# A 96-byte tile at the right edge of the on-chip memory, ahead of all pools on that side

## The chip, the cores and the metric

The kernel runs on one core of a Trainium2 chip. The metric is the device time of one execution in microseconds, lower is better. A core has a matrix engine (PE, with the loading of its stationary operand shown apart as PEld), a vector engine (DVE), a scalar engine (ACT), GpSimd (POOL) and SyncE (SP), whose queue issues nearly all DMAs here. The on-chip memory has 128 partitions; a tile takes the same byte range in each of them. The program's allocator gives out this range from both ends: pools opened on the left grow upwards, pools opened with `side="right"` are stacked downwards from the right edge.

## What is computed

Three layers in a row, in float32 (the weights of the second layer arrive as float64):

```python
attn_out = _attn_ref(q, k, v, centroids)        # 2 batches, 8 heads, 768 tokens, head size 64;
                                                # a query sees only keys of the same nearest centroid
x = attn_out.transpose(0, 2, 1, 3).reshape(1536, 512)
x = (sigmoid(x @ w_gate) * (x @ w_val)) @ w_out # 512 -> 1536 -> 512
p = domain_probs / (domain_probs.sum(-1, keepdims=True) + 1e-09)
out = sum(p[:, e:e+1] * (relu(x @ w1[e]) @ w2[e]) for e in range(4))   # 512 -> 1024 -> 512
```

## The kernel before

**Attention** (to about 290 us) runs over 96 items: 8 pairs of heads, each with 2 heads of 6 tiles of 128 queries. The order of all work is written out by hand (`SLOT`, `START`, `FIRST`, `TAIL`). For each item PE forms the scores `S` (L420), DVE their negated maximum (L423), ACT the exponentials `P` (L431), PE transposes `P` (`T`, L440), ACT and DVE split it in a high and a low part `ph` and `pl` (L443, L444), and PE multiplies these with `vv` (`PV`, L453 and L454). Between the items the next pair is prepared: `nq`, `nk`, `nv` are loaded, q and k are transposed (L243) and split in `hiq`, `loq`, `hik`, `lok`, which DMAs on the SP queue copy to the tiles `L` and `R` of the scores (L378 to L383).

**Gated MLP** (to about 574 us). Every float32 product is made of three passes by `mm3` (L620 to L622): high weights with high x, high weights with low x, low weights with high x. The weights are the stationary operand, 128 columns of 4 bytes, and x is the moving one. `gate` makes `pg` and `pv` from the weights `wgh`, `wgl`, `wvh`, `wvl` and the moving `X0`, `X1`: for the first two f-tiles in four pieces of 384 tokens, for the ten others in three pieces of 512 tokens. `outp` makes `po` from the stationary `woh`, `wol` and the moving `hh`, `hl`, 512 columns wide.

**Mixture** (to the end). For each of 32 f-tiles `hidden` makes three blocks `ph` of 512 tokens, 12 products each, from the stationary `w1h`, `w1l` and the moving `X0`, `X1` (which now hold the MLP's result). After each four f-tiles `outp` makes 12 blocks `po` of 12 products each, from the stationary `h2h`, `h2l` and the moving `woh`, `wol` (L802 to L804). PE takes the products in the order of the program; the weights of the coming f-tiles are loaded and split by ACT and POOL two f-tiles ahead (L762 to L765, L613, L614).

**Where the tiles lie.** On the left side: `X0`, `X1`, the constants, `L`, `R`, `P`, `ph`, `pl`, `vv`, `U`, and later `acc`, `sg`, `woh`, `wol`, `hh`, `hl`, `h2h`, `h2l`. On the right side, all through `self.right`: the pools `nat` (`nq`, `nk`, `nv`), `hl` (`hiq` and its like) and `pm` in attention; `raw` (float64 weights), `cv` and `whl` (`wgh`, `wgl`, `wvh`, `wvl`) in the MLP; `raw2` and `w1p` (`w1h`, `w1l`) in the mixture. The right edge is at byte 229,344 of a partition, which is 1,791 x 128 + 96. The matrix operands have these start addresses in the program before (the slices that one product takes start a multiple of 512 bytes further on):

| operand | role | starts at byte | left over by 128 | left over by 512 |
|---|---|---|---|---|
| `X0`, `X1` | moving | 16,768 and 41,344 | 0 | 384 |
| `woh`, `wol` | stationary in the MLP, moving in the mixture | 94,592 to 113,024 | 0 | 384 |
| `hh`, `hl`, `h2h`, `h2l` | moving in the MLP, stationary in the mixture | 115,072 to 170,368 | 0 | 384 |
| `wgh`, `wgl`, `wvh`, `wvl` | stationary | 184,288 to 198,624 | 96 | 480 |
| `w1h`, `w1l` | stationary | 208,864 to 219,104 | 96 | 480 |
| `P` (transposes) | stationary | 121,728 to 127,872 | 0 | 384 |
| `nq`, `nk` (transposes) | stationary | 220,128 and 223,200 | 96 | 480 |

In attention the left pools end at byte 183,168 and the lowest right pool begins at 183,264, so that 96 bytes are free between them.

Of the kernel before, what the change touches and what calls it, by code (L numbers as in the profile page):

```python
# [5 lines left out]
F32 = mybir.dt.float32  # L6
# [17 lines left out]
BIG = float(2.0 ** 100)  # L24
CLOW, CHIGH = 2.0, float(15 * 2 ** 29)  # bits 0x40000000 and 0x4FF00000: exponents 0 and 255 after the shift

# [4 lines left out]

# The item of a pair of heads (12 to a pair) at which a piece of its work is issued, and where within the item:
# 0 after the scores, 1 after the products with v, 2 at the end.
SLOT = {
# [7 lines left out]
AHEAD, PVLAG = 2, 2  # L42
# The engines that split parts of q, k and v.
ON = {"q0": "pool", "q1": "dve", "k0": "mix", "k1": "dve", "vhi": "act"}
# What comes before the first item: steps of the first two pairs (as pair and step), and the first items' scores.
START = [
# [5 lines left out]
]  # L52
# Items of the other steps of these two pairs that don't keep to the table.
FIRST = {
# [3 lines left out]
}  # L58
# The same, counted from the end of attention, for the first weights of the gated MLP: room, loads, steps of conversion.
TAIL = {  # L60
# [8 lines left out]
class Net:  # L69
# [37 lines left out]
    def warm(self, n):  # L107
        """Products that nobody reads: the array's clock falls to half while it waits."""
        ps = self.ps.tile([128, 384], F32, name="PV", tag="PV", bufs=1)
        for _ in range(n):  # L110
            self.nc.tensor.matmul(ps[:, 0:128], self.identb, self.identb, start=True, stop=True)

    def centroids(self, p):
        """Normalised centroids, transposed, split and laid out as the weights of the similarities."""
        nc = self.nc
        x = p.tile([128, D], F32, name="cx")
        nc.scalar.dma_start(out=x, in_=self.cent.rearrange("h c d -> (h c) d"))
        xx = p.tile([128, 2 * D], F32, name="cxx")

        def scale():  # L120
            sx = p.tile([128, D], F32, name="csx")
            nc.vector.tensor_tensor(sx, x, x, op=ALU.mult)
            sq = p.tile([128, 1], F32, name="csq")
            nc.vector.tensor_reduce(sq, sx, axis=AX.X, op=ALU.add)
            r = p.tile([128, 1], F32, name="cr")
            nc.gpsimd.tensor_tensor(r, sq, self.half[:, 0:1], op=ALU.pow)
            nc.vector.tensor_scalar(r, r, 1e-6, None, op0=ALU.add)
            nc.vector.reciprocal(r, r)
            nc.vector.tensor_scalar(xx[:, 0:D], x, r, None, op0=ALU.mult)
            nc.vector.tensor_scalar(xx[:, D:2 * D], x, r, None, op0=ALU.mult)  # L130

        def place():
            ps = self.ps.tile([128, 128], F32, name="cT", tag="T", bufs=3)
            nc.tensor.transpose(ps, xx, self.ident)
            ch = p.tile([128, 128], F32R, name="ch")
            cl = p.tile([128, 128], F32R, name="cl")
            nc.scalar.activation(ch, ps, AF.Copy)
            nc.vector.tensor_tensor(cl, ps, ch.bitcast(F32), op=ALU.subtract)
            for hh in range(2):
                rows = slice(hh * 64, hh * 64 + 64)  # L140
                for part, src in ((0, ch), (1, cl)):
                    sv = src[rows].bitcast(F32).rearrange("p (a h c) -> p a h c", a=4, h=2)[:, :, hh, :]
                    for s in range(2):
                        o = part * 64 + s * 32 + hh * 16
                        (nc.vector if part else nc.gpsimd).tensor_copy(self.cb[rows, :, s, o:o + 16], sv)

        return scale, place
# [12 lines left out]

# [1 line left out]
    def load_nat(self, src, b, pr, tag):  # L162
# [6 lines left out]
    def prep(self, n):  # L169
        """What pair n needs before its scores, as (item at which it is issued, work) in order."""  # L170
        nc = self.nc
        b, pr = self.plist[n]
        P = self.pairs[n] = {}
        first = n == 0
        x, hl = {}, {}
# [5 lines left out]

        # 1 / (norm + 1e-6) of the rows of q and k
        def square(s, m):
# [37 lines left out]
        def vsplit(hh):  # L221
            def go():
                # v as [Vh0 | Vl0 | Vl1 | Vh1]
                if hh == 0:
                    P["vv"] = self.vvp.tile([128, NT, 4, 64], F32R, name="vv", tag="vv")
                hi, lo = P["vv"][:, :, 3 * hh, :], P["vv"][:, :, 1 + hh, :]
                xv = x["v"][:, :, hh * 64:hh * 64 + 64]
                if ON["vhi"] == "act":
                    nc.scalar.activation(hi, xv, AF.Copy)
                else:  # L230
                    nc.vector.tensor_copy(hi, xv)
                nc.gpsimd.tensor_tensor(lo, xv, hi.bitcast(F32), op=ALU.subtract)
            return go
# [88 lines left out]
        def arg_first(hh):  # L322
            """The same for one head of the first pair, which nothing hides: in small pieces."""
            G = NT * 2
# [121 lines left out]
    def pv(self, n, hh, th, ph, pl):  # L446
        """One half of a head's tokens, in three pieces."""
        nc = self.nc
# [12 lines left out]
        if th == 1:  # L461
            # the two products with the halves of v meet on the head's rows
            if hh == 0:
                P["A"] = self.xsp.tile([128, S], F32, name="A", tag="A")
                P["W"] = self.xsp.tile([128, S], F32, name="W", tag="W")
            r, o = slice(hh * 64, hh * 64 + 64), slice(64 - hh * 64, 128 - hh * 64)
            nc.sync.dma_start(out=P["A"][r], in_=U[r])
            nc.sync.dma_start(out=P["W"][r], in_=U[o])

    def finish(self, n):  # L470
# [22 lines left out]

        # the vector engine has less to do once the last scores are through
        eng = nc.vector if n == len(self.plist) - 1 else nc.gpsimd
# [73 lines left out]

# [1 line left out]
    def conv64(self, raw, tag, hl_pool, put):  # L571
        """float64 bits in raw (int64) -> float32 rounded to nearest even, split in two; as steps to issue in turn."""
        nc = self.nc
        shape = list(raw.shape)
        n = shape[1] * shape[2]
# [4 lines left out]
        def magnitude():  # L580
            # a factor of 2^16 on the high word's bits as a float32 moves the exponent's bias to that of float32
            t["c"] = self.cv.tile([128, n], I32, name="cvc", tag="cvc")
            t["s"] = self.cv.tile([128, n], I32, name="cvs", tag="cvs")
            nc.scalar.activation(t["c"].bitcast(F32), hi_w.bitcast(F32), AF.Abs, scale=float(2.0 ** 16))
            nc.scalar.activation(t["s"], lo_w.bitcast(U32), AF.Copy, scale=float(2.0 ** -29))
# [31 lines left out]
    def mm3(self, ps, wh, wl, xh, xl, first, last):  # L617
        """ps += w.T @ x, float32 products from three float32r passes."""
        nc = self.nc
        nc.tensor.matmul(ps, wh, xh, start=first, stop=False)  # L620
        nc.tensor.matmul(ps, wh, xl, start=False, stop=False)  # L621
        nc.tensor.matmul(ps, wl, xh, start=False, stop=last)  # L622

# [1 line left out]
    def open_weights(self):  # L625
# [21 lines left out]
    def moe1(self):  # L647
# [61 lines left out]

        # the tokens of the first batch go first: the last pair of heads is still under way  # L710
        half = [slice(i * 384, i * 384 + 384) for i in range(4)]
# [37 lines left out]

# [1 line left out]
    def open_mixture(self):  # L751
# [6 lines left out]
    def prepare(self, i):  # L758
        """Weights of the i-th f-tile of the mixture."""
        e, f = self.tiles[i]  # L760
# [6 lines left out]
    def moe2(self):  # L767
# [20 lines left out]
        def outp(ch):  # L788
            first, last = ch == 0, ch == len(tiles) // CH - 1
            e = tiles[ch * CH][0]  # L790
            for t in range(B * NT):
                # the very last product is halved, to end sooner
                parts = (slice(0, 256), slice(256, 512)) if last and t == B * NT - 1 else (slice(0, 512),)
# [28 lines left out]
    def run(self):  # L822
# [4 lines left out]
        self.X = [self.xp.tile([128, 4, N], F32R, name=n, tag=n) for n in ("X0", "X1")]  # L827
        self.dr = es.enter_context(self.tc.tile_pool(name="dr", bufs=2, space=DRAM))
        self.right = es.enter_context(ExitStack())
        with ExitStack() as a:  # L830
            self.psS = self.pool(a, "psS", 2, PSUM)
            self.ps = self.pool(a, "ps", 1, PSUM)
            # what only the preparation of a pair uses gives way to the first weights before the last pair ends
            self.nat = self.pool(self.right, "nat", 1, side="right")
# [62 lines left out]
```

## Time and profile before

| | |
|---|---|
| time, median of 3 runs | 1111.92 us (1109.7 to 1115.82) |
| span of the profiled execution | 1109.4 us |
| time of the profiled execution beside its span | not recorded for this kernel; the fastest run lies 0.3 us above the span, the median 2.5 us |
| PE busy | 1083.7 us, 98% of the span |
| PE's weight loads busy | 920.5 us, 83% |
| DVE, ACT, POOL busy | 551.5, 425.7 and 313.9 us |
| granted PE clock, mean | 0.995 of full speed |

Products on PE overlap: a row says how long one took from its start to its modelled end, while the next one starts well before. What the stream costs is the distance from start to start, which a timeline gives: the difference of two starts divided by the number of products between them.

### The profile page before, as it was taken

To read this page: it belongs to the slowest core of one execution; us is meant where nothing else is said; L and a number is where in the kernel's file an instruction comes from. 1 tells how busy PE (TensorE), PEld (TensorE's weight loads), DVE (VectorE), ACT (ScalarE), POOL (GpSimd) and SP (SyncE) were. 2 spreads that over 40 slices of the span, in tenths; PEclk is the share of its full clock that TensorE was granted. 3 is DMA by queue.
4 is the path that set the end of the run, shared out by engine and by line. 5 is a ranking of instruction groups with operands and counts; after the bars stand their busy time and mean duration, and the time that the engine had idled before them with its cause. 6 is when DMAs were issued, how large, how long until landed. Compare 5 with 4: busy or idle time off the path is not lost.

```text
span 1109.4 us, 14146 instructions
## 1 busy us (share of the span) xinstructions
PE 1083.7 (98%) x5387; PEld 920.5 (83%) x5387; DVE 551.5 (50%) x887; ACT 425.7 (38%) x866; POOL 313.9 (28%) x267
## 2 busy tenths in 40 slices
PE   6999999998999999999999999999999999999998
PEld 5998999998988888888888888888888888888887
DVE  7999999999776355534342222222222222222222
ACT  4887888888565035404232022120211202021110
POOL 7577778834232012102021021110202102021100
PEclk8999999999999999999999999999999999999999
DMA  7677766655342112102011010010101101010002
GB/s 172 143 160 160 175 149 154 149 131 147 115 133 97 37 43 94 36 1 86 10 36 31 19 48 29 19 48 10 58 19 39 38 1 58 19 48 10 10 19 95
DMA packets 88515, 78.94 MB, mean 71 GB/s; under 512 B 42720, under 2 KB 71744, under 8 KB 88448
## 3 DMA queue, kind: packets, MB, share of 16 engines
q1 hardware_dynamic: 88016, 77.99, 27.2%
q8 instruction: 42, 0.69, 0.3%
q14 instruction: 25, 0.20, 0.1%
q10 hardware_dynamic: 432, 0.06, 0.0%
HBM read 48.29 MB, written 3.19 MB: 46 GB/s over the span
## 4 chain that ended last, share of the span: by engine, by line
PE 89%; DVE 4%; DMA 4%; SPq 1%; issue 1%; ACT 1%; POOL 0%; ACTq 0%; POOLq 0%; DVEq 0%
PE ph L620 8%; PE ph L621 8%; PE ph L622 8%; PE po L804 8%; PE po L803 8%; PE po L802 8%; PE T L440 4%; PE S L420 4%; PE po L622 3%; PE po L620 3%; PE po L621 3%; PE pg L620 3%; PE pv L622 3%; PE pg L621 3%; PE pv L621 3%; PE pv L620 3%
## 5 line engine op out<-in xcount | busy, mean ns | idle before, releaser
L785 DVE SCALAR_TENSOR_TENSOR h2l<-ph,h2h 128x512 fp32r<-128x512 f32 x96 | 66.4, 691 | 208.9 <-ACT h2h L784 208.9
L620 PE MATMUL ph<-X,w1h 128*128 128x512 f32 x384 | 152.3, 396 | 0.0
L621 PE MATMUL ph<-X,w1h 128*128 128x512 f32 x384 | 152.2, 396 | 0.0
L622 PE MATMUL ph<-X,w1l 128*128 128x512 f32 x384 | 152.2, 396 | 0.0
L802 PE MATMUL po<-woh,h2h 128*128 128x512 f32 (+1 forms) x388 | 150.1, 387 | 0.0
L803 PE MATMUL po<-wol,h2h 128*128 128x512 f32 (+1 forms) x388 | 150.1, 387 | 0.0
L804 PE MATMUL po<-woh,h2l 128*128 128x512 f32 (+1 forms) x388 | 150.1, 387 | 0.0
L809 DVE SCALAR_TENSOR_TENSOR acc<-po,pn,acc 128x512 f32<-128x512 f32 (+1 forms) x85 | 63.3, 744 | 159.1 <-PE po L804 159.1
L614 POOL TENSOR_TENSOR wol<-r,woh 128x512 fp32r<-128x512 f32 x32 | 41.5, 1306 | 271.1 <-ACT woh L613 224.8
L613 ACT ACTIVATE woh<-r 128x512 fp32r<-128x512 f32 x32 | 20.2, 631 | 240.7 <-PE po L804 207.7
L595 POOL TENSOR_TENSOR cvc<-cvc,cvs 128x512 int32<-128x512 int32 x36 | 50.3, 1401 | 202.4 <-DVE cvc L592 196.4
L444 DVE TENSOR_TENSOR pl<-T,ph 128x384 fp32r<-128x384 f32 x192 | 96.9, 545 | 11.9 <-ACT ph L443 10.3
L784 ACT ACTIVATE h2h<-ph 128x512 fp32r<-128x512 f32 x96 | 56.8, 591 | 109.8 <-PE ph L622 109.7
L614 POOL TENSOR_TENSOR w1l<-r,w1h 128x512 fp32r<-128x512 f32 x32 | 41.8, 1307 | 181.4 <-ACT w1h L613 179.2
L420 PE MATMUL S<-R,L 80*128 80x384 f32 (+1 forms) x384 | 91.4, 360 | 0.7 <-ACT P L431 0.7
L443 ACT ACTIVATE ph<-T 128x384 fp32r<-128x384 f32 x192 | 84.4, 492 | 19.8 <-PE T L440 19.0
L423 DVE TENSOR_REDUCE nm<-S 128x1 f32<-128x768 f32 x96 | 90.9, 947 | 1.9 <-PE S L420 1.0
L431 ACT ACTIVATE P<-S,nm 128x768 f32<-128x768 f32 x96 | 87.4, 911 | 4.3 <-DVE nm L423 4.3
L440 PE MATMUL T<-ident,P 128*128 128x128 f32 x576 | 82.5, 277 | 5.0 <-DVE pl L444 4.5
L622 PEld LDWEIGHTS ph<-X,w1l 128*128 128x128 f32 x384 | 72.3, 188 | 17.7
L620 PEld LDWEIGHTS ph<-X,w1h 128*128 128x128 f32 x384 | 72.3, 188 | 17.6
L621 PEld LDWEIGHTS ph<-X,w1h 128*128 128x128 f32 x384 | 72.3, 188 | 17.6
(164 smaller groups left out, 2108.2 us busy)
## 6 DMA issues: line engine op xcount, KB each, us to landing
r<-in_moe_w_dram SPq DMA_DIRECT2D x64, 256.0 KB, 2.7
L<-hiq SPq DMA_DIRECT2D x32, 192.0 KB, 4.7
R<-hik SPq DMA_DIRECT2D x32, 192.0 KB, 4.7
wo<-in_moe_w_out_dram SPq DMA_DIRECT2D x12, 512.0 KB, 3.5
wv<-in_moe_w_val_dram SPq DMA_DIRECT2D x12, 512.0 KB, 3.8
wg<-in_moe_w_gate_dram SPq DMA_DIRECT2D x12, 512.0 KB, 4.2
nq<-in_q_dram SPq DMA_DIRECT2D x16, 192.0 KB, 3.6
nk<-in_k_dram SPq DMA_DIRECT2D x16, 192.0 KB, 3.7
```

The costliest lines, as they stand in the source:

```text
L420: nc.tensor.matmul(ps[:, a, 0:384], l[0:k, c], r[0:k, a * 384:a * 384 + 384], start=l is L1, stop=l is L2)
L423: nc.vector.tensor_reduce(nm, ps[:, :, 0:384], axis=AX.XY, op=ALU.max, negate=True)
L431: nc.scalar.activation(r2(pt), ps[:, :, 0:384], AF.Exp, bias=nm, scale=1.0, accum_out=P["sums"][:, i:i + 1])
L440: nc.tensor.transpose(ps[:, j, :], pt[:, c:c + 128], self.ident)
L443: nc.scalar.activation(hi, ps, AF.Copy)
L444: nc.vector.tensor_tensor(lo, ps, hi.bitcast(F32), op=ALU.subtract)
L620: nc.tensor.matmul(ps, wh, xh, start=first, stop=False)
L621: nc.tensor.matmul(ps, wh, xl, start=False, stop=False)
L622: nc.tensor.matmul(ps, wl, xh, start=False, stop=last)
L802: nc.tensor.matmul(ps, Hh[:, c], wh[:, dc], start=j == 0, stop=False)
L803: nc.tensor.matmul(ps, Hh[:, c], wl[:, dc], start=False, stop=False)
L804: nc.tensor.matmul(ps, Hl[:, c], wh[:, dc], start=False, stop=j == CH - 1)
```

## The change

A pool `edge` is opened on the right side before all others, with one tile of 24 floats (96 bytes) in each partition, and POOL fills it once with zeros. Nothing reads it. Every pool on the right side moves down by 96 bytes, and with it each of its tiles; none on the left moves. The rest of the diff takes out comments and leaves the line numbers up to L828 as they were.

```diff
@@ -826,11 +826,14 @@
         self.xp = self.pool(es, "xp")
         self.X = [self.xp.tile([128, 4, N], F32R, name=n, tag=n) for n in ("X0", "X1")]
         self.dr = es.enter_context(self.tc.tile_pool(name="dr", bufs=2, space=DRAM))
+
+        edge = self.pool(es, "edge", side="right").tile([128, 24], F32, name="edge")
+        self.nc.gpsimd.memset(edge, 0.0)
         self.right = es.enter_context(ExitStack())
         with ExitStack() as a:
```

## Rows read from the trace of the kernel before

**Rows 1.** The page: span, and PE's busy time.

```profile
span 1109.4 us, 14146 instructions
...
PE 1083.7 (98%) x5387; PEld 920.5 (83%) x5387; DVE 551.5 (50%) x887; ACT 425.7 (38%) x866; POOL 313.9 (28%) x267
```

**Rows 2.** Windows: stretch, us; PE, PEld, DVE, ACT, POOL busy; clock, DMA, GB/s.

```profile
31.00:283.00 252.00, 241.93 (x1633) 229.50 (x1632) 232.11 (x390) 214.35 (x499) 162.16 (x126) 0.99 0.67 154
...
300.00:574.00 274.00, 274.00 (x1197) 224.16 (x1196) 143.70 (x230) 98.22 (x169) 46.49 (x34) 1.00 0.17 54
```

**Rows 3.** Groups by form on PE: busy us, mean ns of one.

```profile
L620 PE MATMUL ph<-X,w1h 128*128 128x512 f32 x384 | 152.3, 396 | 0.0
...
L802 PE MATMUL po<-woh,h2h 128*128 128x512 f32 x380 | 147.9, 389 | 0.0
...
L620 PE MATMUL pg<-X,wgh 128*128 128x512 f32 x120 | 47.6, 397 | 0.0
```

**Rows 4.** Timeline of PE, mixture: start us, us of one.

```profile
574.27 0.39 PE L620 MATMUL ph<-X,w1h 128*128 128x512 f32 x1
...
616.44 0.40 PE L802 MATMUL po<-woh,h2h 128*128 128x512 f32 x1
...
649.09 0.39 PE L620 MATMUL ph<-X,w1h 128*128 128x512 f32 x1
```

**Rows 5.** Timeline of PE, gated MLP: pieces of 384, then of 512 tokens.

```profile
281.55 0.34 PE L620 MATMUL pg<-X,wgh 128*128 128x384 f32 x1
...
285.71 0.34 PE L620 MATMUL pg<-X,wgh 128*128 128x384 f32 x1
...
407.76 0.40 PE L620 MATMUL pg<-X,wgh 128*128 128x512 f32 x1
...
424.63 0.39 PE L620 MATMUL pg<-X,wgh 128*128 128x512 f32 x1
```

**Rows 6.** Timeline of PE, the last change from `ph` to `po`.

```profile
1072.62 0.39 PE L802 MATMUL po<-woh,h2h 128*128 128x512 f32 x1
...
1074.01 0.39 PE L802 MATMUL po<-woh,h2h 128*128 128x512 f32 x1
```

**Rows 7.** Groups by form on PEld, the weight loads.

```profile
L802 PEld LDWEIGHTS po<-woh,h2h 128*128 128x128 f32 x388 | 72.9, 188 | 14.9
...
L620 PEld LDWEIGHTS ph<-X,w1h 128*128 128x128 f32 x384 | 72.3, 188 | 17.6
...
L440 PEld LDWEIGHTS T<-ident,P 128*128 128x128 f32 x576 | 67.2, 141 | 12.6 <-DVE pl L444 7.4 <-ACT R L365 0.6 <-issue 0.2
...
L243 PEld LDWEIGHTS T<-ident,nq 128*128 128x128 f32 x48 | 6.2, 142 | 0.5
```

**Rows 8.** Groups by form, other engines: mean ns, idle before, releaser.

```profile
L785 DVE SCALAR_TENSOR_TENSOR h2l<-ph,h2h 128x512 fp32r<-128x512 f32 x96 | 66.4, 691 | 208.9 <-ACT h2h L784 208.9
...
L614 POOL TENSOR_TENSOR w1l<-r,w1h 128x512 fp32r<-128x512 f32 x32 | 41.8, 1307 | 181.4 <-ACT w1h L613 179.2 <-DMA r<-in_moe_w_dram 2.3
L614 POOL TENSOR_TENSOR wol<-r,woh 128x512 fp32r<-128x512 f32 x32 | 41.5, 1306 | 271.1 <-ACT woh L613 224.8 <-PE po L621 46.1
```

**Rows 9.** Waits: PE from 290 us on; ACT in attention.

```profile
PE pg L620 <- ACT sg L676: 0.9, 1, 0.9
...
ACT hik L252 <- DMA R<-hik: 6.1, 5, 1.6
```

**Rows 10.** DMA issues: count, KB each, median us to landing.

```profile
L<-hiq SPq DMA_DIRECT2D x32, 192.0 KB, 4.7
...
W<-U SPq DMA_DIRECT2D x16, 192.0 KB, 4.6
```

**Rows 11.** Timeline of POOL and of DVE from the start.

```profile
0.73 0.20 POOL masks.py:197 MEMSET ident<- 128x128 f32 x1 [0.29 <-POOLq L881]
...
2.14 0.59 POOL L105 MEMSET desc<- 128x1 f32 x16
...
1.34 1.48 DVE L94 CAST identb<-ident 128x128 bf16<-128x128 f32 x1 [0.45 <-POOL ident masks.py:199]
```

## The prediction

> **What bounds the kernel now.** I read the page first: PE is busy for 98% of the span [rows 1], so a change that touches no work of PE has little to win. The table by stretches then separates the layers [rows 2]. In attention PE, DVE and ACT are all busy for most of the time (241.9, 232.1 and 214.4 of 252 us), the DMA engines for 67% of it. In the gated MLP PE is busy for all 274.0 us of the stretch while DVE, ACT and POOL are at 143.7, 98.2 and 46.5, with the clock granted in full (1.00, the 2.4 GHz level). The waits say the same: from 290 us to the end PE waited for another engine once, 0.9 us [rows 9]. So from there on the time is the sum of the distances between the starts of PE's products, and a change has to shorten these.
>
> The third view is the timeline, for these distances. In the mixture the first `ph` starts at 574.27 and, 5 f-tiles or 180 products later, the first `po` at 616.44: 42.17 / 180 = 234.3 ns each. The 144 `po` products that follow end where `ph` starts again, at 649.09: 32.65 / 144 = 226.7 ns [rows 4]. Both stream 512 columns through 128 x 128 weights of 4 bytes, at the same clock, and yet differ by 7.5 ns. In the MLP the 512-wide products of `gate` cost as much as `ph`: 72 of them from 407.76 to 424.63 give 234.3 ns [rows 5]. The groups by form show the same step in what one product takes: 396 and 397 ns for `ph` and `pg`, 389 for `po` [rows 3].
>
> What do the slow ones share? By the table of addresses their stationary operand lies on the right side, 480 beyond a multiple of 512 bytes, and their moving operand is `X`. The quick ones have everything on the left, at 384 beyond a multiple of 512. 128 x 4 bytes are 512, and 512 x 4 bytes are 2,048: all slices of one operand begin at the same place within 512.
>
> **The change part by part.** *The weights on the right.* They move to 384 beyond a multiple of 512, exactly where the operands of the quick `po` begin; `X` was there all along. If the place of the weights is what costs 7.5 ns, all products of that kind drop from 234.3 to 226.7. There are 3 x 384 = 1,152 `ph` products, and 6 groups of 120 in `pg` and `pv`, 720 products of 512 columns [rows 3]. The sum: 1,152 x 7.54 ns = 8.69 us, and 720 x 7.57 ns = 5.45 us (234.31 less 226.74), together 14.1 us. The 192 products of `gate` that are 384 wide get nothing: 24 of them took 285.71 - 281.55 = 4.16 us, 173.3 ns each [rows 5], and this is what the quick kind would cost at that width: 226.7 less 128 columns at 2.4 GHz (53.3 ns) is 173.4.
>
> Bounds of this term: the low end is nothing. The high end is the same 14.1 us, as no 512-wide product of the trace goes below 226.7. Between the ends I take the high one, since it is the row with the same operands' places.
>
> *Is there cover for a quicker PE?* A block of 12 products would take 2.72 us in place of 2.81. DVE needs 0.69 us for a block of `ph`, and POOL 1.31 + 1.31 us for the weights of a whole f-tile, 36 products or 8.2 us [rows 8]; in the MLP the busiest helper, DVE, stands at 143.7 of 274 us [rows 2]. Nothing of this is late when 3% go.
>
> *Other readers and writers of the right side.* POOL subtracts weights whose result lies on the right (`w1l`) in 1307 ns and on the left (`wol`) in 1306 [rows 8]; the side doesn't show, so I take nothing for DVE, ACT and POOL. The transposes of q, with their data 480 beyond 512, load in 142 ns, those of `P` on the left in 141 [rows 7]: 96 transposes of q and k at 1 ns are 0.1 us, taken as nothing.
>
> *DMAs out of the right side.* The copies to `L` and `R` start from moved rows; their destinations stay. `L<-hiq` lands in 4.7 us, `W<-U`, of the same size and wholly on the left, in 4.6 [rows 10]. ACT waits 6.1 us in all for such copies [rows 9]. So the ends are 6.1 us won, were they to vanish from the path, and 0.1 us lost for each of 7 prepared pairs, 0.7 us, were the shift to cost the difference of these rows. I take nothing, nearest to the 0.1.
>
> *The new instruction.* POOL zeroes 24 floats in each partition before `ident`, for which DVE's `identb` and PE's first products wait. 128 floats take 0.20 us and 16 single columns 0.59 us, 0.04 each [rows 11]. So it costs 0.04 to 0.20 us at the head of the kernel; I take 0.05. The tile is read by nobody, and the 96 bytes it takes were free.
>
> Sum: 1109.4 - 14.1 + 0.05 = 1095.3 us of span. The median of the runs shown lies 2.5 us above the profiled span, which gives **1097.8 us**.
>
> **The rivals.** *Half of it.* One of the two pools gains and the other not, as they hold other addresses above the lowest 512 bytes: with the MLP alone 1111.9 - 5.4 = 1106.5 us, with the mixture alone 1111.9 - 8.7 = 1103.2. For: nothing in the trace ties the two together. Against: today they show the same 234.3.
>
> *Nothing happens.* The extra 7.5 ns belongs to `X` as the moving operand, or to its being read at this width, and the weights' place is innocent: 1111.9 us, and the spread of the runs around it. For this speak three rows. The same weights at the same addresses cost no extra under 384 columns [rows 5]. The load itself is shown with the same 188 ns for `w1h` and for `h2h`, and a load from an odd place is no longer in the transposes either [rows 7]. And after the last `ph` the extra lives on for a while with every operand on the left: the first six `po` products from 1072.62 to 1074.01 still have 231.7 ns [rows 6], so that it isn't a plain price of each load. Against it speaks that `X` begins at the same place within 512 as `hh` and `woh`, and only its distance from the other operands is special; the place of the weights is the one low address that differs. The Trainium skill has a rule on this rival's side: the page SBUF — State Buffer, section Door 1: The DMA port swizzle, gives the memory 16-byte lines and charges an access for crossing to a new one. 96 is a multiple of 16, so by this rule weights at 96 and at 0 beyond 128 cost the same, and the time would stay at 1111.9; no row here shows a line of any size.
>
> *Slower.* Today the two streams that PE reads, weights and moving data, begin 96 bytes apart within 512; afterwards they begin at the same place. If that makes them meet where now they pass each other, the 1,872 products lose where I let them win: by the same 7.5 ns, the time is 1111.9 + 14.1 = 1126.0 us. It decides from 3 ns a product on (5.6 us, 0.5%). Against: `po` runs in exactly that position, in both layers, at 226.7 [rows 4].
>
> **How the numbers follow.** All of it 0.66, half 0.08, nothing 0.20, slower 0.06. What a measurement of this kernel can tell from no change is about 0.5%, 5.6 us; half of it in either form is near or over that bound, so I count it as faster: faster 0.74, same 0.20, slower 0.06. The likeliest case's own range is 1094 to 1101 us: the span plus 0.3 to 6.4 us, as the runs lie above it now, less a part of the 6.1 us of waits. To leave out no more than two in ten, the range for all cases reaches down to 1093 and up to 1112, to the middle of the case in which nothing happens: 0.64 of the first, 0.08, and 0.10 of the third.
>
> **What would show it.** In the timeline after, `ph` must go from f-tile to f-tile in 36 x 226.7 = 8.16 us in place of 8.43, `pg` and `pv` likewise, and `po` must stay at 226.7 in the MLP and the mixture. The groups by form should give 389 ns to `ph` and `pg`. The 384-wide pieces should stay at 173.3 and the copies to `L` and `R` near 4.7 us. Attention should end where it ends now, the MLP take 5.4 us less and the mixture 8.7 less. If `ph` stays at 234.3, the weights' place was not the cause, and the choice fell wrong between `X` and the weights. If `ph` drops and the span doesn't, another engine has become late, and DVE in the MLP would be the first to look at.

## The result and the profile after

The changed kernel takes 1096.07 us (median of 4 runs, 1094.5 to 1098.44) against 1111.01 us of the kernel before in the same comparison. The ratio is 0.9861, with a 95% interval from 0.9842 to 0.988: faster by 1.4%, and clear of the 0.5% that can be told from no change. The forecast was 1097.8 us, and 1095.3 us for the profiled span, which is 1095.2.

The page after: the span, and PE's busy time, against [rows 1].

```profile
span 1095.2 us, 14147 instructions
...
PE 1071.5 (98%) x5387; PEld 921.3 (84%) x5387; DVE 551.3 (50%) x887; ACT 426.1 (39%) x866; POOL 313.9 (29%) x268
```

The groups by form on PE after, against [rows 3]: busy us, mean ns of one.

```profile
L620 PE MATMUL ph<-X,w1h 128*128 128x512 f32 x384 | 149.4, 389 | 0.0
...
L620 PE MATMUL pg<-X,wgh 128*128 128x512 f32 x120 | 46.7, 389 | 0.0
```

The timeline of PE after, with the starts that answer to [rows 4, 5]: a 384-wide `pg`, the first 512-wide one, two starts that are 72 such products apart, then the mixture.

```profile
299.48 0.33 PE L620 MATMUL pg<-X,wgh 128*128 128x384 f32 x1
...
307.80 0.39 PE L620 MATMUL pg<-X,wgh 128*128 128x512 f32 x1
...
405.76 0.39 PE L620 MATMUL pg<-X,wgh 128*128 128x512 f32 x1
...
422.08 0.39 PE L620 MATMUL pg<-X,wgh 128*128 128x512 f32 x1
...
568.96 0.39 PE L620 MATMUL ph<-X,w1h 128*128 128x512 f32 x1
...
609.76 0.39 PE L802 MATMUL po<-woh,h2h 128*128 128x512 f32 x1
...
642.40 0.39 PE L620 MATMUL ph<-X,w1h 128*128 128x512 f32 x1
```

72 products of `gate` now take 422.08 - 405.76 = 16.32 us, 226.7 ns each (234.3 before), 180 of `ph` 40.80 us, 226.7 each (234.3), and 144 of `po` 32.64 us, 226.7 as before. The 384-wide pieces take (307.80 - 299.48) / 48 = 173.3 ns, also as before. One row of the kernel before places the gain by layer, the start of its first 512-wide `pg`:

```profile
307.64 0.39 PE L620 MATMUL pg<-X,wgh 128*128 128x512 f32 x1
```

From there to the first `ph` it took 574.27 - 307.64 = 266.6 us before and 568.96 - 307.80 = 261.2 after, 5.5 less. The mixture took 1109.4 - 574.3 = 535.1 and takes 1095.2 - 569.0 = 526.2, 8.9 less. What precedes is 0.2 us longer.

The start of POOL after, against [rows 11], shows the new instruction. It is put ahead of `ident`, which starts 0.05 us later:

```profile
0.73 0.12 POOL L831 MEMSET edge<- 128x24 f32 x1 [0.29 <-POOLq L884]
0.78 0.20 POOL masks.py:197 MEMSET ident<- 128x128 f32 x1
```

PE's waits from 290 us on are the same 0.9 us as before, and `L<-hiq` lands in 4.6 us (4.7 before).

So the time came from where it was forecast. What this doesn't show is why. Three theories fit before and after alike: (1) the stationary operand must lie at a multiple of 128 bytes, (2) the two operands of a product must lie at matching places, (3) neither may lie off a multiple of 128. The experiments tell them apart. Below, *difference* is the place of the moving operand less that of the stationary one, left over by 512.

### The profile page after: what moved, and what is told of

It reads as the page before. It is cut to its first block, busy times and chain, and to the rows that moved or that the text cites. A ratio compares the mean times of both kernels' runs of the same rounds, so it can differ in the third digit from the quotient of the medians.

```text
span 1095.2 us, 14147 instructions
## 1 busy us (share of the span) xinstructions
PE 1071.5 (98%) x5387; PEld 921.3 (84%) x5387; DVE 551.3 (50%) x887; ACT 426.1 (39%) x866; POOL 313.9 (29%) x268
## 4 chain that ended last, share of the span: by engine, by line
PE 87%; DVE 6%; DMA 3%; ACT 2%; issue 1%; SPq 1%; POOL 0%; ACTq 0%; POOLq 0%; DVEq 0%
PE po L803 8%; PE ph L621 8%; PE po L804 8%; PE po L802 8%; PE ph L620 8%; PE ph L622 8%; PE T L440 4%; PE S L420 4%; PE po L620 3%; PE po L622 3%; PE po L621 3%; PE pg L620 3%; PE pv L620 3%; PE pg L621 3%; PE pg L622 3%; PE pv L621 3%
## 5 line engine op out<-in xcount | busy, mean ns | idle before, releaser
L620 PE MATMUL ph<-X,w1h 128*128 128x512 f32 x384 | 149.4, 389 | 0.0
L621 PE MATMUL ph<-X,w1h 128*128 128x512 f32 x384 | 149.4, 389 | 0.0
L622 PE MATMUL ph<-X,w1l 128*128 128x512 f32 x384 | 149.4, 389 | 0.0
L614 POOL TENSOR_TENSOR w1l<-r,w1h 128x512 fp32r<-128x512 f32 x32 | 42.1, 1316 | 172.0 <-ACT w1h L613 172.0
L802 PEld LDWEIGHTS po<-woh,h2h 128*128 128x128 f32 x388 | 72.9, 188 | 14.9
L803 PEld LDWEIGHTS po<-wol,h2h 128*128 128x128 f32 x388 | 72.9, 188 | 14.8
L804 PEld LDWEIGHTS po<-woh,h2l 128*128 128x128 f32 x388 | 72.9, 188 | 14.8
```

The lines of the kernel that those rows point to most:

```text
L802: nc.tensor.matmul(ps, Hh[:, c], wh[:, dc], start=j == 0, stop=False)
L803: nc.tensor.matmul(ps, Hh[:, c], wl[:, dc], start=False, stop=False)
L804: nc.tensor.matmul(ps, Hl[:, c], wh[:, dc], start=False, stop=j == CH - 1)
```

## Experiments

**Smaller tiles at the edge.** In the first the edge tile has 32 bytes, in the second 64.

```diff
-        edge = self.pool(es, "edge", side="right").tile([128, 24], F32, name="edge")
+        edge = self.pool(es, "edge", side="right").tile([128, 8], F32, name="edge")    # second: [128, 16]
```

> The edge tile is 32 bytes in place of 96, so that all tiles on the right side lie 64 beyond a multiple of 128 bytes. If a multiple of 64 is enough for the weights, ph and the 512-wide pg and pv have 226.7 ns from start to start and the time is about 1096 us, as with 96 bytes. If it takes a multiple of 128, they stay at 234.3 ns and the time at about 1111 us.

> The edge tile is 64 bytes, so that the right side lies 32 beyond a multiple of 128 (and of 64). If a multiple of 64 or of 128 is what counts, ph, pg and pv have 234.3 ns and the time is about 1111 us, though a tile of nearly the same size is put at the edge. If what counts is only the old place, 96 beyond 128, they have 226.7 ns and the time is 1096 us.

Measured: 1111.35 us with 32 bytes, ratio to before 0.9983 (0.9972 to 0.9995), and 1110.5 us with 64 bytes, 0.9974 (0.9958 to 0.999). Both are within 0.5% of the kernel before. Two starts of the run with 32 bytes, 180 `ph` products apart, in its timeline of PE, then the same of the run with 64 bytes:

```profile
575.31 0.40 PE L620 MATMUL ph<-X,w1h 128*128 128x512 f32 x1
...
617.30 0.39 PE L802 MATMUL po<-woh,h2h 128*128 128x512 f32 x1
```

```profile
574.66 0.39 PE L620 MATMUL ph<-X,w1h 128*128 128x512 f32 x1
...
616.65 0.39 PE L802 MATMUL po<-woh,h2h 128*128 128x512 f32 x1
```

41.99 / 180 = 233.3 ns; with 64 bytes it is 41.99 us for 180 as well (574.66 to 616.65). So neither a tile at the edge as such nor a multiple of 64 bytes does it. Two more starts of the run with 32 bytes, 48 of the 384-wide products apart, hold a surprise:

```profile
300.82 0.34 PE L620 MATMUL pg<-X,wgh 128*128 128x384 f32 x1
...
309.30 0.40 PE L620 MATMUL pg<-X,wgh 128*128 128x512 f32 x1
```

8.48 / 48 = 176.7 ns: here the narrow pieces lose 3.3 ns, which they didn't in the kernel before.

**One layer's weights alone.** In the changed kernel, ahead of the right pools of the mixture:

```diff
     def open_mixture(self):
         self.right.close()
+        pad = self.pool(self.right, "pad", side="right").tile([128, 8], F32, name="pad")
+        self.nc.gpsimd.memset(pad, 0.0)
         self.raw = self.pool(self.right, "raw2", 2, side="right")
```

> The changed kernel, with 32 bytes more put above the right pools of the mixture alone: w1h and w1l lie 96 beyond 128 again, 352 beyond 512 in place of 480, and the weights of the gated MLP stay at a multiple of 128. Theory 1 (the place of the stationary operand costs 7.5 ns a product): ph 234.3 ns, pg and pv 226.7, time 1096.1 + 8.7 = 1104.8 us. Rival (one common cause for the whole right side, as a shift of the copies of attention or of the loads): both products alike, time 1096 or 1111 us.

Measured: 1106.53 us (1102.05 to 1107.22), ratio to before 0.9929 (0.9906 to 0.9952), span 1102.3. The timeline of PE, 288 products of `gate`, then 180 of `ph`:

```profile
389.39 0.39 PE L620 MATMUL pg<-X,wgh 128*128 128x512 f32 x1
...
454.67 0.39 PE L620 MATMUL po<-hh,woh 128*128 128x512 f32 x1
...
568.92 0.39 PE L620 MATMUL ph<-X,w1h 128*128 128x512 f32 x1
...
610.91 0.39 PE L804 MATMUL po<-woh,h2h 128*128 128x512 f32 x1
```

`ph` takes 41.99 / 180 = 233.3 ns, the gated MLP's products 65.28 / 288 = 226.7. The loss follows the one layer's weights. Over the span after, 1102.3 - 1095.2 = 7.1 us, against 1,152 x 6.6 = 7.6; the median of the five runs, which lie 5 us apart, is 10.5 us above that of the changed kernel.

**The operands of `po`.** In the changed kernel, on the left side, only `hh`, `hl`, `h2h`, `h2l` move, by 96 bytes:

```diff
+        pad = self.pool(es, "pad").tile([128, 24], F32, name="pad")
+        self.nc.gpsimd.memset(pad, 0.0)
         self.hp = self.pool(es, "hp", 5)
```

> The changed kernel, with 96 bytes put in on the left side ahead of the pool hp: hh, hl, h2h, h2l lie 96 beyond 128, all else at multiples of 128. In the gated MLP they are the moving operand of po, in the mixture the stationary one. Theory 1 (only the stationary operand's place counts): po stays at 226.7 ns in the MLP (432 products) and goes to 234.3 in the mixture (about 1,150 products of 512 columns), time 1096.1 + 8.7 = 1104.8 us. Theory 2 (what counts is that the two operands lie at different places within 128) and theory 3 (either operand off a multiple costs): 234.3 in both layers, time 1096.1 + 12.0 = 1108.1 us.

Measured: 1108.94 us (1106.94 to 1111.54), ratio to before 0.9962 (0.9947 to 0.9976), span 1107.6. The timeline of PE, `po` of the MLP from its start to the next `pg`, then `po` of the mixture to the next `ph`, 144 products each:

```profile
357.89 0.40 PE L620 MATMUL po<-hh,woh 128*128 128x512 f32 x1
...
391.51 0.40 PE L620 MATMUL pg<-X,wgh 128*128 128x512 f32 x1
...
613.89 0.39 PE L802 MATMUL po<-woh,h2h 128*128 128x512 f32 x1
...
647.62 0.39 PE L620 MATMUL ph<-X,w1h 128*128 128x512 f32 x1
```

33.62 / 144 = 233.5 ns in the MLP, where the moved operand is the moving one, and 33.73 / 144 = 234.2 in the mixture, where it is the stationary one. Theory 1 falls: its stationary `woh` lay where it had been quick.

**Everything off a multiple of 128.** The kernel before, without the edge tile, with 96 bytes on the left ahead of all pools. The right side stays where it was.

```diff
+        pad = self.pool(es, "pad").tile([128, 24], F32, name="pad")
+        self.nc.gpsimd.memset(pad, 0.0)
         self.cpool = self.pool(es, "const")
```

> The kernel before, without the edge tile, with 96 bytes put in on the left side ahead of all pools: every tile on either side lies 96 beyond a multiple of 128, 480 beyond 512, and no operand differs in place from another. Theory 2 (it costs when the two operands lie at different places within 128): all 512-wide products have 226.7 ns, time about 1096 us. Theory 3 (it costs when either operand is off a multiple of 128): all of them, po too, have 234.3 ns or more, time 1111 + 12 = 1123 us or more.

Measured: 1101.1 us (1099.52 to 1102.31), ratio to before 0.9892 (0.9867 to 0.9918). The timeline of PE:

```profile
571.47 0.39 PE L620 MATMUL ph<-X,w1h 128*128 128x512 f32 x1
...
612.27 0.39 PE L802 MATMUL po<-woh,h2h 128*128 128x512 f32 x1
...
644.91 0.39 PE L620 MATMUL ph<-X,w1h 128*128 128x512 f32 x1
```

40.80 / 180 = 226.7 ns for `ph`, 32.64 / 144 = 226.7 for `po`. The weights lie at the very addresses of the kernel before, 96 beyond 128, and the products are quick. This decides for theory 2: the difference counts, not the multiple. (Its median lies 5.0 us above the changed kernel's, the span of its profiled execution, 1097.7, 2.5 us. These 2.5 us all stand ahead of the mixture, where `ph` starts at 571.47 in place of 568.96; the mixture takes 526.2 us in both. What costs more ahead of it is not shown.)

**All at multiples of 128, but not at the same place.** The pad of 96 bytes ahead of `hp` becomes one of 128:

```diff
+        pad = self.pool(es, "pad").tile([128, 32], F32, name="pad")
+        self.nc.gpsimd.memset(pad, 0.0)
         self.hp = self.pool(es, "hp", 5)
```

> The changed kernel with 128 bytes put in ahead of hp in place of 96: hh, hl, h2h, h2l lie at a multiple of 512, woh and wol 384 beyond one; all lie at multiples of 128. If a multiple of 128 is all that counts, po stays at 226.7 ns in both layers and the time at 1096 us. If the operands must lie at the same place within 512, po goes to about 234 ns and the time to 1108 us.

Measured: one run, 1108.06 us, span 1106.3. `po` in its timeline, 144 products from each first row to the second:

```profile
358.76 0.40 PE L620 MATMUL po<-hh,woh 128*128 128x512 f32 x1
...
392.36 0.39 PE L620 MATMUL pg<-X,wgh 128*128 128x512 f32 x1
...
614.63 0.40 PE L802 MATMUL po<-woh,h2h 128*128 128x512 f32 x1
...
648.10 0.39 PE L620 MATMUL ph<-X,w1h 128*128 128x512 f32 x1
```

33.60 / 144 = 233.3 and 33.47 / 144 = 232.4 ns. Every operand lies at a multiple of 128, and `po` is slow.

**More differences.** Two kernels with a pad at three places: above the right pools of the MLP, above those of the mixture, and ahead of `hp`. The first has 256, 64 and 192 bytes, the second 512, 384 and 32.

```diff
     def open_weights(self):
         self.right.close()
+        pad = self.pool(self.right, "pad1", side="right").tile([128, 64], F32, name="pad")    # second: 128
+        self.nc.gpsimd.memset(pad, 0.0)
...
     def open_mixture(self):
         self.right.close()
+        pad = self.pool(self.right, "pad2", side="right").tile([128, 16], F32, name="pad")    # second: 96
+        self.nc.gpsimd.memset(pad, 0.0)
...
+        pad = self.pool(es, "pad0").tile([128, 48], F32, name="pad")    # second: 8
+        self.nc.gpsimd.memset(pad, 0.0)
         self.hp = self.pool(es, "hp", 5)
```

> The changed kernel with three more pads, all multiples of 32 bytes: 256 bytes above the right pools of the gated MLP, 64 above those of the mixture, 192 ahead of hp. Within 512 bytes the moving operand then begins this far after the stationary one: pg and pv 256, ph 64, po of the MLP 192, po of the mixture 320. Theory 2 as the runs so far have shaped it (a 512-wide product is quick only where both operands begin at the same place within 512): all four are slow, 232 to 235 ns, time about 1096 + 20 = 1116 us. Rival (a multiple of 128 between them is enough where it is 256, half of 512): pg and pv 226.7 ns, the others slow, time about 1111 us.

> The same with pads of 512, 384 and 32 bytes: pg and pv have a difference of 0 within 512 at another address than before, ph has 384, po of the MLP 32 and po of the mixture 480. Theory 2: pg and pv 226.7 ns, the other three 232 to 235 ns, time about 1096 + 14 = 1110 us. If any move away from the addresses of the changed kernel costs, pg and pv are slow as well; if a multiple of 128 were enough, ph is quick.

Measured: one run each, 1115.24 us (span 1113.4) and 1112.99 us (span 1111.2). The timeline of PE of the first: 144 `po` of the MLP, 288 of `gate`, then 180 `ph` and 144 `po` of the mixture.

```profile
357.18 0.39 PE L620 MATMUL po<-hh,woh 128*128 128x512 f32 x1
...
390.77 0.39 PE L620 MATMUL pg<-X,wgh 128*128 128x512 f32 x1
...
456.07 0.39 PE L620 MATMUL po<-hh,woh 128*128 128x512 f32 x1
...
572.25 0.40 PE L620 MATMUL ph<-X,w1h 128*128 128x512 f32 x1
...
614.25 0.40 PE L806 MATMUL po<-woh,h2h 128*128 128x512 f32 x1
...
647.85 0.40 PE L620 MATMUL ph<-X,w1h 128*128 128x512 f32 x1
```

`gate`, at a difference of 256, takes 65.30 / 288 = 226.7 ns; the others 233.3. So theory 2 needs a correction: a difference of 256 does as well as one of 0. In the second kernel `gate`, moved by 512 bytes, stays at 226.8 ns, 65.32 us for 288, which clears the move as such; the other three are slow. The rows for `gate`:

```profile
389.60 0.40 PE L620 MATMUL pg<-X,wgh 128*128 128x512 f32 x1
...
454.92 0.40 PE L620 MATMUL po<-hh,woh 128*128 128x512 f32 x1
```

The sum holds in the first: 1,152 `ph`, 1,140 512-wide `po` of the mixture and 432 of the MLP at 6.6 ns more are 18.0 us, and the span is 18.2 above the changed kernel's.

All differences together, in products of 512 columns:

| difference within 512 | ns from start to start | where |
|---|---|---|
| 0 | 226.7 | `po` before; all after; all in the run with 96 bytes on the left; `gate` moved by 512 |
| 32 | 233.3 | `ph` with 32 bytes in the mixture; `po` of the MLP with 32 |
| 64 | 233.3 | `ph`, first of the last two |
| 96 | 233.5 | `po` of the MLP with 96 bytes ahead of `hp` |
| 128 | 233.3 | `po` of the MLP with 128 |
| 192 | 233.3 | `po` of the MLP with 192 |
| 256 | 226.7 | `gate`, first of the last two |
| 320 | 233.3 | `po` of the mixture with 192 |
| 384 | 232.4 and 233.3 | `po` of the mixture with 128; `ph`, second of the last two |
| 416 | 234.3 and 234.2 | `ph` and `gate` before; `po` of the mixture with 96 |
| 448, 480 | 233.3 | `ph` with edge tiles of 32 and 64 bytes |

**Other widths.** The 1,536 tokens of a hidden f-tile in other pieces, once in the kernel before and once in the changed one:

```diff
-            for blk in range(3):
-                c = slice(blk * 512, blk * 512 + 512)
-                ps = self.ps2.tile([128, 512], F32, name="ph", tag=("pg", "pv")[blk % 2])
+            w, end = (384, 416, 448, 480)[i % 4], 0
+            for blk in range(4):
+                c = slice(end, min(end + w, N))
+                end = c.stop
+                ps = self.ps2.tile([128, 512], F32, name="ph", tag=("pg", "pv")[blk % 2])[:, 0:c.stop - c.start]
```

> The kernel before, weights on the right 96 beyond 128, with the 1,536 tokens of a hidden f-tile cut in pieces of 384, 416, 448 or 480 (and what is left over), in turn over the f-tiles. It asks from which width on the weights' place costs, since gate showed nothing at 384 columns. If the extra grows with the width, ph has 173.3 ns at 384 and a few ns more than the same piece of the changed kernel at 416, 448 and 480, reaching 7 ns towards 512. If it is a property of the full 512 columns alone, all four widths cost the same as in the changed kernel. po stays at 226.7 ns.

> The changed kernel with the same cut of the hidden f-tiles: the reference for the run with the odd place. By the row of 384 columns (173.3 ns) and that of 512 (226.7) each further column costs 0.417 ns: 186.7 ns at 416, 200.0 at 448 and 213.3 at 480.

Measured: one run each, 1121.87 us and 1113.18 us; these kernels issue a third more products in `hidden`. The expectation took the changed kernel for quick at every width, and it isn't. Its timeline of PE, 12 products from each row to the next of the same width:

```profile
653.51 0.37 PE L620 MATMUL ph<-X,w1h 128*128 128x448 f32 x1
...
656.00 0.37 PE L620 MATMUL ph<-X,w1h 128*128 128x448 f32 x1
...
662.27 0.40 PE L620 MATMUL ph<-X,w1h 128*128 128x480 f32 x1
...
664.90 0.37 PE L620 MATMUL ph<-X,w1h 128*128 128x480 f32 x1
...
667.46 0.38 PE L620 MATMUL ph<-X,w1h 128*128 128x480 f32 x1
```

The first piece of 448 begins at a difference of 0 and takes 2.49 us / 12 = 207.5 ns, some 7 above the 200.0 expected. The first piece of 480, also at 0, takes 219 ns, and the second, which begins 1,920 bytes on, at a difference of 384, takes 213, the quick value. With the odd place the second piece of 480, at a difference of 288, has 220 ns (672.81 to 675.45). Over all products of a kind in both kernels' traces, 448 columns take 206 to 207 ns at each of the four differences that occur (0, 160, 256, 416); 480 columns take 214 at 384 and 218 to 220 at the five others (0, 160, 256, 288, 416). So which difference is quick depends on the width; the table above is for 512 columns. As to what the experiment asked, the odd place costs next to nothing when `hidden` is cut this way: its 1,536 products take 277.4 us with it and 276.5 without, where the 512-wide ones of the two kernels differ by 8.7.

**The same place in attention.** In the changed kernel, the pool `sm` moves behind `xsp`, so that `ph` and `pl` of attention move down by its 1,280 bytes and begin at the same place within 512 as `vv`, which stays (`P`, `U` and the tiles of `xsp` move down with them):

```diff
-            self.sm = self.pool(a, "sm", 2)
...
             self.xsp = self.pool(a, "xsp", 1)
+            self.sm = self.pool(a, "sm", 2)
```

> The changed kernel with the pool sm, 1,280 bytes in size, moved behind xsp on the left side, so that vv, ph and pl of attention begin at the same place within 512 (128, where now vv is at 128 and ph and pl at 384). No byte more, no instruction changed. Theory 2 carried to 384 columns: the products of PV with ph go from 178 to 173.3 ns, 192 x 4.7 ns = 0.9 us, of which only a part lies on the path of attention: 1095 to 1096 us. Rival (at 384 columns the place doesn't matter, as the pieces of gate showed for a difference of 96): 178 ns and the time stay.

Measured: 1098.73 us (1094.46 to 1099.04), ratio to the kernel before 0.9876 (0.9852 to 0.9901), which overlaps that of the changed kernel. The groups by form of this run:

```profile
L453 PE MATMUL PV<-ph,vv 128*128 128x384 f32 x192 | 66.6, 347 | 4.7 <-ACT U L460 4.7
L454 PE MATMUL PV<-pl,vv 128*128 128x384 f32 x192 | 65.0, 339 | 0.0
```

The changed kernel has 348 and 340 ns. From start to start, two rows of this run that are three products apart:

```profile
100.54 0.34 PE L453 MATMUL PV<-ph,vv 128*128 128x384 f32 x1
...
101.07 0.34 PE L454 MATMUL PV<-pl,vv 128*128 128x384 f32 x1
```

0.53 us for three, as in the changed kernel (101.48 to 102.01), and the middle distance from a product with `ph` to the one with `pl` behind it is 178 ns in both. The rival holds: nothing is won here. The two differences compared are 256 before and 0 now, which are both quick at 512 columns, so that this run says nothing against the table.

## Why the prediction was right, point by point

*The bound.* From the gated MLP on the time is the sum of the distances between PE's products: right. Summed in the two traces, the 1,152 and 720 products take 8.73 and 5.43 us less, against 8.69 and 5.45 forecast, and make up nearly all of the 8.9 and 5.5 us that the two layers gained.

*The step from the slow kind to the quick kind.* Right in its size and in the products it named, since the operands were compared with those of `po` down to the last 512 bytes. The words for it, that the place of the weights is what costs, were too narrow, though the time came out: in this layout the weights reach their new place and the place of `X` in one move, so that the number could not tell the two readings apart. The run with all operands off a multiple of 128 has the weights at their old place and is quick; the runs with 96 and 128 bytes ahead of `hp` have unmoved weights in the MLP and are slow. What counts is the place of the two operands to each other. The change helps because `X` was at 384 within 512 and the edge tile brings the weights there; that this is a multiple of 128 is a coincidence.

*Cover, other engines, DMAs.* Right: PE's waits from 290 us on stayed at 0.9 us, DVE's `h2l` at 692 ns (691), the copies at 4.6 us. POOL's `w1l` took 1316 ns (1307), which is hidden.

*The new instruction.* 0.05 us, as taken.

*From span to median.* The forecast of the span, 1095.3 us, was met to 0.1. The 2.5 us put on top were too much: each of the four runs lies 1.7 to 1.8 us above its own span, and the median here 0.9 above the profiled one.

*Half of it.* Didn't happen; both layers gained in full. The run with only the mixture's weights moved shows that the two parts are separate.

*Nothing happens.* Fell, though what spoke for it is half of the truth: the extra did belong to `X` as much as to the weights. The row of the 384-wide pieces, which was read as the weights being innocent, was a case of its own: at this width a difference of 416 costs nothing, one of 448 costs 3.3 ns. The change from `ph` to `po` in [rows 6], read as the extra living on, is one of two among eight in that trace that show it past the first `po`; at the six others the first `po` has 226 to 228 ns. The rule of 16-byte lines from the Trainium skill (SBUF — State Buffer, section Door 1: The DMA port swizzle) would have had weights at 96 and at 0 beyond 128 cost the same. With `X` where it was, they differ by 7.6 ns a product here, and those at 32 and 64 from 0 by 6.6, all multiples of 16; the measurement decides.

*Slower.* Fell with its sign turned round: products whose operands begin at the same place within 512 are among the quickest, at 512 columns.

What stays open: the mechanism. The runs give the pattern, not what inside PE or the memory makes it. Nor do they say why the extra lives on for some products at some changes of operands and not at others, or which differences are quick at further widths.

Open too is which weights are the partner of the moving operand. While one product streams, the trace shows the weights of the next one being loaded, here in the run with 32 bytes in the mixture, where the last `po` gives way to `ph`:

```profile
643.32 0.40 PE L806 MATMUL po<-woh,h2l 128*128 128x512 f32 x1
643.33 0.19 PEld L620 LDWEIGHTS ph<-X,w1h 128*128 128x128 f32 x1
```

All weights of one stream lie at the same place within 512, so the table can't tell a product's own weights from the next one's; only the changes between streams can. In this run the last `po` ahead of `ph`, with its own weights at a difference of 0 and the next ones at 32, takes 234 to 235 ns to the next start in all eight cases, and the last `ph` ahead of `po`, with 32 and 0, takes 225 to 227 in all eight (in the trace's nanoseconds, finer than the rows). So there the price goes with the weights that are being loaded. Other runs are less clean: with 32 bytes at the edge, the last `po` ahead of `ph` takes 226 to 227 ns, though the next weights are at 448, and the first `ph` 236. It is a hint, not shown.

## What to carry to other kernels

Where products of one shape have different distances from start to start in one trace, compare the addresses of their operands, both of them, before looking for a wait; the engine's 98% busy time hides the 3%, and of a duration of 390 ns it is 7 [rows 3]. With 512-wide float32r products and 128 x 128 weights, lay moving and stationary tiles out so that their start addresses differ by a multiple of 256 bytes; being aligned to 64 or 128 is neither needed nor enough. A before-and-after pair can't tell an absolute place from a relative one: move the other operand.

## What the runs showed of the hardware that was not expected

The distance between products depends on where the moving operand and the weights of its stream lie to each other: 226.7 ns at a difference of 0 or 256 bytes within 512, and 232.4 to 234.3 ns at the ten others tried, with all operands at multiples of 32 bytes and a granted clock of 1.00 in these stretches.

The effect has its own dependence on width: at 384 columns 173.3 ns at differences of 0, 416 and 480 and 176.7 at 448; at 480 columns 213 at 384 and 219 at 0.
